# Key splits of an attention and MoE kernel: from a planner's choice of three engines to ScalarE and VectorE

## The chip, the cores and the metric

The kernel runs on one core of a Trainium2 chip. The metric is device time in microseconds (us) from one launch; the profile adds one execution with a record of every instruction. A core has TensorE (PE, matrix products; PEld is its loading of weights), VectorE (DVE), ScalarE (ACT), GpSimd (POOL) and SyncE (SP), each with its own queue of instructions, which it works off in order. SP here does nothing but issue DMAs.

## What is computed

An attention with a learned bias, followed by two feed-forward layers. The part that the change touches, cut down:

```python
scores = q @ k.T / 8                                   # 2 batches x 8 heads, 576 x 576, head size 64
x = log1p(abs(i - j)) / log1p(max(i, 1))               # for each query i and key j
bias = relu(x * w1 + b1) @ w2                          # 32 hidden units, one bias for each head
attn = softmax(scores + bias)
out = attn @ v
# then: two layers g(x @ w_in) @ w_out on 1152 tokens, model size 512, inner size 2048
```

All is float32. Where the kernel multiplies in the fp32r format of TensorE, it splits a number into a first part (rounded to fp32r) and a remainder, and adds up the products of the parts.

## The kernel before

**Stages.** One loop over steps from -16 to 83 issues the attention. In each step, functions that were put on a list for that step (`at` for a fixed engine, `flex` for a choice of engines) are issued by priority; the matrix products and the DMAs of a step come last. Then a second loop issues the two feed-forward layers. The order on every engine is thus written out ahead; the engines wait for one another by semaphores alone.

**The planner.** `flex` gives a cost for each engine that may do a piece of work (V is VectorE, A ScalarE, G GpSimd). `pick` (line 99) takes the engine whose load plus that cost is lowest, and adds the cost to the load. At the head of each step `run_step` (line 107) lowers each load by a pace (0.846 before step 0, 1.791 from it on), not below zero. A load that is carried along therefore shifts later choices too.

**Bias rows.** `bias_rows` (line 184) makes the bias for groups of 16 query rows. `relu` computes four hidden tiles of 128 x 576 (VectorE line 208, or ScalarE line 206), `mm` multiplies them by w2 on TensorE (line 219, eight products), `evac` brings the result from PSUM to a buffer (`copy`, ScalarE line 134 or VectorE line 142), and `store` sends it off by DMA. The first twelve groups ("near", the ones with start steps up to 2) fill two SBUF tiles `bias0`; the other 24 go through DRAM (`bd`) and have shorter tiles. There are nine buffers for hidden tiles, and two PSUM buffers for the first eight groups, which the score tiles share.

**Key splits.** `split_k` (line 275) does this for each of 8 heads and 2 batches: `hi` copies 64 partitions x 576 of the raw keys to fp32r (GpSimd line 144, ScalarE line 134 or VectorE line 138), and in the next step `lo` subtracts that copy from the raw keys (GpSimd or VectorE, line 149) and writes the remainder to the other 64 partitions. The raw keys come in four DMAs (`kraw`). `split_q` does the like for the queries, by the planner's choice on GpSimd.

**Scores.** From step 0 on, one tile of 128 queries and one head per step: TensorE makes the scores (line 364), VectorE adds the bias and takes the minimum of the negated scores (line 373), ScalarE takes exp (line 378), VectorE the reciprocal of the sum, GpSimd multiplies by it (`norm`, line 146), TensorE transposes (line 404), ScalarE copies that out of PSUM, and TensorE multiplies by v (lines 417 and 420). In the late steps weights of the feed-forward layers are split as well (`conv`, stages s0 to s4, lines 492 to 520).

Of the kernel before, what the change touches and what calls it, by code (L numbers as in the profile page):

```python
# [27 lines left out]
def f(ap):  # L28
    return ap.bitcast(F32)
# [5 lines left out]
def near_row(pr, m):  # L35

    return 64 * (pr // 4) + pr % 4 + 4 * m


class Kernel:  # L40
# [50 lines left out]
    def at(self, step, eng, fn, pri=0, cost=0.3):  # L91

        self.todo.setdefault(step, []).append((pri, eng, fn, cost))
# [90 lines left out]
    def bias_rows(self, pr, s0, p, ps, pss, cfg):  # L184


        nc = self.nc
        V, A, G, at = nc.vector, nc.scalar, nc.gpsimd, self.at
        i0 = 16 * pr
        near = pr < 12  # L190
        d = S if near else max(S - i0, i0 + 16)
        nh = 1 if d <= 512 else 2
        w = d // nh
        one = near and PAR["order"].index(pr) < PAR["ns"]
        st = {}
        hid = []
        c0 = i0 + 15

        def relu(e, j):
            t = p.tile([128, S], F32, tag="hid", name="hid", bufs=cfg["hid"])  # L200
            hid.append(t)
            thr = self.thr[:, 4 * pr + j:4 * pr + j + 1]
            o = 188 - near_row(pr, 4 * j)
            u = self.us[:, o:o + S] if near else self.u
            if e == "A":
                A.activation(t[:, :d], u[:, :d], AF.Relu, bias=thr)
            else:
                V.tensor_scalar(t[:, :d], u[:, :d], thr, 0.0, ALU.add, ALU.max)  # L208

        def mm(x):  # L210
            if one:
                if x == 0:
                    st["s"] = pss.tile([128, 2, 512], F32, tag="s", name="bps2", bufs=2)
                st[x] = st["s"][:, x]
            else:
                st[x] = ps.tile([128, 512], F32, tag="T", name="bps", bufs=3)
            w2 = self.w2s.rearrange("p i h -> p (i h)")
            for j in range(4):
                nc.tensor.matmul(st[x][32 * j:32 * j + 32, :w], lhsT=w2, rhs=hid[j][:, x * w:x * w + w],  # L219
                                 start=True, stop=True, tile_position=(0, 32 * j))  # L220

        def evac(e, x):
            if x == 0:
                st["buf"] = p.tile([128, BW], F32, tag="bbuf", name="bbuf", bufs=PAR["bbuf"])
            buf = st["buf"]
            if one:
                self.copy(e, buf[:, 0:d].rearrange("p (x c) -> p x c", x=2), st["s"][:, :, :w], self.rpsi[:, pr:pr + 1])
                return
            dst = buf[:, 0:d] if near else buf[:, c0:c0 + d] if i0 < 288 else buf[:, 0:d][:, ::-1]
            self.copy(e, dst[:, x * w:x * w + w], st[x][:, :w], self.rpsi[:, pr:pr + 1])  # L230

        n = c0 if i0 < 288 else 575 - i0

        def mirror(e):
            buf = st["buf"]
            if i0 < 288:
                self.copy(e, buf[:, 0:n], buf[:, c0 + 1:c0 + 1 + n][:, ::-1])
            else:
                self.copy(e, buf[:, c0 + 1:c0 + 1 + n], buf[:, c0 - n:c0][:, ::-1])

        def store():
            if near:
                for b in (0, 64) if pr < 4 else (64 * (pr >= 8),):
                    nc.sync.dma_start(self.bias0[pr >= 4][b + pr % 4:b + 64:4], st["buf"][:, 0:S])
                return
            bk, r = divmod(pr - 4, 8)
            dst = self.bd[bk][16 * r:16 * r + 16].rearrange("i h c -> (i h) c")
            nc.sync.dma_start(dst[:, 0:591], st["buf"][:, 0:591])

        for j in range(4):  # L250
            self.flex(s0, dict(V=PAR['rV'] + 0.52e-3 * d, A=PAR['rA'] + 0.83e-3 * d), lambda e, j=j: relu(e, j), PAR['vp'][6])
        for x in range(nh):
            g = 0 if one else x
            at(s0 + 1 + g, "P", lambda x=x: mm(x), PAR["pp"][1])
            if not one or x:
                v = d if one else w
                self.flex(s0 + (PAR["evd"][pr] if near else 2) + g, dict(V=0.13 + 1.04e-3 * v, A=0.1 + 0.83e-3 * v),
                          lambda e, x=0 if one else x: evac(e, x), PAR['vp'][7])
        if near:
            at(s0 + PAR["evd"][pr] + g, "end", store)  # L260
            return
        self.flex(s0 + 3 + g, dict(G=PAR['mG'] + 1e-3 * n, V=PAR['mV'] + 0.52e-3 * n, A=PAR['mA'] + 0.83e-3 * n), mirror, PAR['vp'][8])
        at(s0 + 4 + g, "end", store)
# [11 lines left out]
    def split_k(self, h, sl, s0, p, K, tag, bufs):  # L275


        nc, at = self.nc, self.at
        mine = slice(64 * (h % 2), 64 * (h % 2) + 64)
        other = slice(64 - 64 * (h % 2), 128 - 64 * (h % 2))  # L280

        def load():
            self.kraw[h // 2] = p.tile([128, B, S], F32, tag=tag, name="kraw", bufs=bufs)
            nc.sync.dma_start(self.kraw[h // 2], self.a["kc"][h // 2])

        def hi(e, b):
            self.copy(e, K[h][mine, b], self.kraw[h // 2][mine, b])

        def lo(e, b):
            self.sub(e, K[h][other, b], self.kraw[h // 2][mine, b], f(K[h][mine, b]))  # L290

        if h % 2 == 0:
            at(sl, "end", load, -1)
        for b in range(B):
            self.flex(s0 + b, dict(G=PAR['kG'], A=PAR['kA'], V=PAR['kV']), lambda e, b=b: hi(e, b), PAR['pe_'][4])
            self.flex(s0 + b + 1, dict(G=PAR['k2G'], V=PAR['k2V']), lambda e, b=b: lo(e, b), PAR['pe_'][4])

    def ring(self, name):

# [575 lines left out]
```

## Time and profile before

| | |
|---|---|
| median of 3 runs | 626.24 us (625.48 to 626.54) |
| profiled execution, its own time | 623.83 us |
| span of its records | 621.8 us |
| busy in the span | PE 590.9, DVE 514.9, ACT 411.5, POOL 408.1 us |

The span runs from the first to the last record. The profiled execution is a run of its own, so its time differs from the median of the others.

### The profile page before, as it was taken

To read this page: it belongs to the slowest core of one execution; us is meant where nothing else is said; L and a number is where in the kernel's file an instruction comes from. 1 tells how busy PE (TensorE), PEld (TensorE's weight loads), DVE (VectorE), ACT (ScalarE), POOL (GpSimd) and SP (SyncE) were. 2 spreads that over 40 slices of the span, in tenths; PEclk is the share of its full clock that TensorE was granted. 3 is DMA by queue.
4 is the path that set the end of the run, shared out by engine and by line. 5 is a ranking of instruction groups with operands and counts; after the bars stand their busy time and mean duration, and the time that the engine had idled before them with its cause. 6 is when DMAs were issued, how large, how long until landed. Compare 5 with 4: busy or idle time off the path is not lost.

```text
span 621.8 us, 11331 instructions
## 1 busy us (share of the span) xinstructions
PE 590.9 (95%) x4084; PEld 538.0 (87%) x4084; DVE 514.9 (83%) x963; ACT 411.5 (66%) x888; POOL 408.1 (66%) x427
## 2 busy tenths in 40 slices
PE   4679999999989879999999999999999999999997
PEld 1247777677878779999999999999999999999997
DVE  7998898989769779799999987999997699594432
ACT  4478787888778689888887877744754454543330
POOL 5867666686769468688999877665665476295220
PEclk9899999999999889999999999999999999999999
DMA  6876336665454302132212111232232122010012
GB/s 209 218 196 203 113 116 189 229 213 162 163 193 154 137 4 69 34 103 71 100 69 102 69 67 35 72 113 87 78 126 74 64 101 102 2 69 1 14 52 89
DMA packets 26888, 66.25 MB, mean 107 GB/s; under 512 B 4689, under 2 KB 6609, under 8 KB 26833
## 3 DMA queue, kind: packets, MB, share of 16 engines
q1 hardware_dynamic: 26688, 65.44, 32.1%
q8 instruction: 32, 0.52, 0.3%
q14 instruction: 24, 0.19, 0.1%
q10 hardware_dynamic: 144, 0.10, 0.1%
HBM read 51.19 MB, written 9.62 MB: 98 GB/s over the span
## 4 chain that ended last, share of the span: by engine, by line
PE 71%; DVE 16%; DMA 6%; issue 2%; ACT 2%; POOL 0%; SPq 0%; DVEq 0%; ACTq 0%; POOLq 0%
PE outps L733 30%; PE inps L690 29%; DVE hid L208 5%; PE tps L404 3%; PE vps L420 3%; PE sps L364 3%; PE bps L219 3%; DMA bias<-bd 3%; DVE P L373 2%; DVE wc L498 2%; DMA raw<-w 1%; DVE wc L502 1%; DVE K L149 1%; DMA qraw<-qt 1%; PE vps L417 1%
## 5 line engine op out<-in xcount | busy, mean ns | idle before, releaser
L733 PE MATMUL outps<-gh,wo 128*128 128x384 f32 x768 | 209.5, 335 | 0.0
L596 POOL TENSOR_TENSOR gl<-v,gh 128x384 fp32r<-128x384 f32 x96 | 110.0, 1147 | 79.0 <-ACT gh L592 74.5
L733 PEld LDWEIGHTS outps<-gh,wo 128*128 128x128 f32 x768 | 139.8, 188 | 0.0
L733 PE MATMUL outps<-gl,wo 128*128 128x384 f32 x384 | 128.3, 334 | 0.0
L690 PE MATMUL inps<-x,wh 128*128 128x384 f32 x384 | 100.4, 343 | 3.3 <-DVE x L439 2.0
L146 POOL TENSOR_SCALAR P<-P,m 128x576 f32<-128x576 f32 x72 | 59.6, 831 | 34.9 <-DVE m L383 25.2
L690 PEld LDWEIGHTS inps<-x,wh 128*128 128x128 f32 x384 | 70.7, 192 | 4.3 <-DVE x L439 2.3
L733 PEld LDWEIGHTS outps<-gl,wo 128*128 128x128 f32 x384 | 72.1, 188 | 0.0
L559 ACT ACTIVATE v<-inps,cst 128x384 f32<-128x384 f32 x48 | 27.8, 579 | 66.4 <-PE inps L690 63.5
L378 ACT ACTIVATE P<-P,m 128x576 f32<-128x576 f32 x72 | 56.1, 779 | 21.6 <-DVE m L373 21.2
L583 DVE SCALAR_TENSOR_TENSOR v<-v 128x384 f32<-128x384 f32 x48 | 39.8, 829 | 33.9 <-ACT v L559 33.6
L690 PE MATMUL inps<-x2l,wh 128*128 128x384 f32 x192 | 64.6, 337 | 1.6 <-DVE x2l L666 1.6
L563 POOL TENSOR_TENSOR q<-h,q 128x384 f32<-128x384 f32 x48 | 48.8, 1016 | 26.1 <-ACT q L556 25.7
L364 PE MATMUL sps<-K,Q 128*128 128x288 f32 x320 | 60.2, 314 | 5.6 <-DVE m L373 5.6
L690 PE MATMUL inps<-x,wl 128*128 128x384 f32 x192 | 65.3, 340 | 0.0
L690 PE MATMUL inps<-x2h,wh 128*128 128x384 f32 x192 | 64.7, 337 | 0.0
L690 PE MATMUL inps<-x2h,wl 128*128 128x384 f32 x192 | 64.5, 336 | 0.0
L592 ACT ACTIVATE gh<-v 128x384 fp32r<-128x384 f32 x96 | 50.7, 528 | 20.4 <-DVE v L584 19.2
L219 PE MATMUL bps<-hid,w2s 128*32 128x288 f32 (+17 forms) x416 | 48.8, 478 | 14.2 <-DVE hid L208 12.5
L502 DVE SCALAR_TENSOR_TENSOR wc<-raw,wc 128x512 int32<-128x512 int32 x64 | 61.3, 968 | 0.0
L373 DVE CUSTOM_DVE_ANT_0 P<-sps,bias 128x576 f32<-128x576 f32 x72 | 53.3, 747 | 9.1 <-DMA bias<-bd 6.6
L364 PEld LDWEIGHTS sps<-K,Q 128*128 128x128 f32 x320 | 45.0, 189 | 9.6 <-DVE m L373 5.7
(87 smaller groups left out, 1305.3 us busy)
## 6 DMA issues: line engine op xcount, KB each, us to landing
raw<-w SPq DMA_DIRECT2D x64, 512.0 KB
bd<-bbuf SPq DMA_DIRECT2D x24, 295.5 KB
bias<-bd SPq DMA_DIRECT2D x24, 288.0 KB
bias<-bbuf SPq DMA_DIRECT2D x16, 288.0 KB
qraw<-qm SPq DMA_DIRECT2D x16, 256.0 KB
V<-v SPq DMA_DIRECT2D x8, 320.0 KB
kraw<-kc SPq DMA_DIRECT2D x4, 576.0 KB
out<-acc SPq DMA_DIRECT2D x12, 192.0 KB
```

The costliest lines, as they stand in the source:

```text
L146: nc.gpsimd.tensor_scalar(out, x, scale, 1.0, ALU.mult, ALU.mult)
L219: nc.tensor.matmul(st[x][32 * j:32 * j + 32, :w], lhsT=w2, rhs=hid[j][:, x * w:x * w + w], start=True, stop=True, tile_position=(0, 32 * j))
L364: PE.matmul(x_[:, x, :288], lhsT=lhs, rhs=K[h][:, bb, 288 * x:288 * x + 288], start=(j == 0), stop=(j == len(seq) - 1))
L373: V.tensor_tensor_reduce(halves(o), S_.pop(t)[:, :, :288], halves(bt), -0.125, 3e38, ALU.add, ALU.min, sums[i][:, 0, e:e + 1])
L378: A.activation(s, s, AF.Exp, bias=m[:, 0, e:e + 1], scale=-1.0, accum_out=m[:, 1, e:e + 1])
L502: return [(dict(V=0.7), lambda e: V.scalar_tensor_tensor(tc, words[:, :, 0], 29, tc, ALU.logical_shift_right, ALU.bitwise_or))]
L563: return [lambda: G.tensor_tensor(o["q"], o["h2"], o["q"], ALU.add)] if m == 0 else []
L583: return [lambda: V.scalar_tensor_tensor(v, v, 1.0, v, ALU.min, ALU.mult), lambda: V.tensor_tensor(v, v, h2, ALU.add)]
L592: return [lambda: A.activation(gh, o["v"], AF.Copy)]
L596: return [lambda: G.tensor_tensor(gl, o["v"], f(o["gh"]), ALU.subtract)]
L690: nc.tensor.matmul(ps[:, :U], lhsT=w[:, c], rhs=y[:, c], start=(t == 0), stop=(t == 11))
L733: nc.tensor.matmul(ps[:, :U], lhsT=w[:, c], rhs=y, start=(t == 0), stop=(t == 11))
```

## The change

The key splits lose their choice of engine: all sixteen `hi` go to ScalarE and all sixteen `lo` to VectorE, each entered in the planner with 0.68. For the relus of groups with a start step of at most 2, which are the twelve near groups, the planner's costs become 0.51 on VectorE and 0.77 on ScalarE, in place of 0.43 and 0.91 (0.13 + 0.00052 x 576 and 0.427 + 0.00083 x 576).

```diff
         for j in range(4):
-            self.flex(s0, dict(V=PAR['rV'] + 0.52e-3 * d, A=PAR['rA'] + 0.83e-3 * d), lambda e, j=j: relu(e, j), PAR['vp'][6])
+            c = dict(V=PAR['rV'] + 0.52e-3 * d, A=PAR['rA'] + 0.83e-3 * d) if s0 > 2 else dict(V=0.51, A=0.77)
+            self.flex(s0, c, lambda e, j=j: relu(e, j), PAR['vp'][6])
...
         for b in range(B):
-            self.flex(s0 + b, dict(G=PAR['kG'], A=PAR['kA'], V=PAR['kV']), lambda e, b=b: hi(e, b), PAR['pe_'][4])
-            self.flex(s0 + b + 1, dict(G=PAR['k2G'], V=PAR['k2V']), lambda e, b=b: lo(e, b), PAR['pe_'][4])
+            self.flex(s0 + b, dict(A=0.68), lambda e, b=b: hi(e, b), PAR['pe_'][4])
+            self.flex(s0 + b + 1, dict(V=0.68), lambda e, b=b: lo(e, b), PAR['pe_'][4])
```

Before, the planner's costs for the splits were G 0.377, A 0.407, V 0.204 for `hi`, and G 1.36, V 0.456 for `lo`.

## Rows read from the trace of the kernel before

**Rows 1.** Windows: start:end and length, busy time (count) by engine, PE clock, DMA share, GB/s.

```profile
4.00:28.00 24.00, 15.05 (x106) 5.36 (x110) 23.53 (x29) 10.14 (x15) 19.76 (x20) 0.93 0.78 216
28.00:49.00 21.00, 17.61 (x158) 9.71 (x155) 20.62 (x40) 16.70 (x37) 13.71 (x20) 1.00 0.79 215
...
53.00:100.00 47.00, 46.65 (x508) 36.17 (x508) 40.62 (x109) 37.41 (x92) 29.68 (x42) 1.00 0.45 153
100.00:162.00 62.00, 60.56 (x576) 44.02 (x575) 54.61 (x144) 49.33 (x120) 42.81 (x57) 1.00 0.55 178
162.00:186.00 24.00, 22.00 (x217) 19.61 (x216) 17.21 (x47) 19.75 (x53) 16.74 (x20) 1.00 0.58 203
186.00:212.00 26.00, 23.74 (x222) 20.76 (x222) 22.66 (x49) 19.34 (x48) 18.07 (x18) 0.98 0.47 159
...
234.00:392.00 158.00, 158.00 (x909) 158.00 (x907) 141.05 (x265) 130.11 (x270) 129.04 (x127) 1.00 0.22 74
```

**Rows 2.** Chain that ended last, 0 to 125 us: start, length, what.

```profile
20.00 3.23 DVE hid L208 x2
...
50.61 2.47 DVE hid L208 x3
...
53.90 0.48 PE tps L404 x3
```

**Rows 3.** Groups by line and shape, 0 to 125 us: count, busy us, mean ns.

```profile
L208 DVE TENSOR_SCALAR hid<-us,thr 128x576 f32<-128x576 f32 x36 | 27.5, 829 | 0.2
L373 DVE CUSTOM_DVE_ANT_0 P<-sps,bias 128x576 f32<-128x576 f32 x37 | 27.4, 746 | 2.6 <-PE sps L364 1.7 <-DMA bias<-bd 0.8
...
L149 POOL TENSOR_TENSOR K<-kraw,K 64x576 fp32r<-64x576 f32 x9 | 13.3, 1475 | 3.0 <-ACT K L134 2.3
...
L144 POOL TENSOR_SCALAR K<-kraw 64x576 fp32r<-64x576 f32 x12 | 10.5, 877 | 6.8 <-DMA kraw<-kc 6.1
L206 ACT ACTIVATE hid<-us,thr 128x576 f32<-128x576 f32 x12 | 9.1, 766 | 4.1 <-DVE thr L176 3.1 <-PE bps L219 1.0
L149 DVE TENSOR_TENSOR K<-kraw,K 64x576 fp32r<-64x576 f32 x7 | 8.5, 1209 | 0.2
...
L134 ACT ACTIVATE bbuf<-bps,small 128x576 f32<-128x576 f32 x8 | 5.9, 740 | 13.5 <-PE bps L219 13.4
...
L149 POOL TENSOR_TENSOR Q<-qraw,Q 128x128 fp32r<-128x128 f32 x8 | 5.1, 657 | 0.0
...
L144 POOL TENSOR_SCALAR Q<-qraw 128x128 fp32r<-128x128 f32 x8 | 3.4, 438 | 1.9 <-DMA qraw<-qt 1.7
...
L134 ACT ACTIVATE K<-kraw 64x576 fp32r<-64x576 f32 x3 | 2.0, 675 | 0.0
...
L142 DVE TENSOR_SCALAR bbuf<-bps,small 128x304 f32<-128x304 f32 x2 | 1.1, 530 | 0.1
```

**Rows 4.** Instructions on the hidden tiles, 0 to 125 us: ns minimum, median, maximum.

```profile
L208 DVE TENSOR_SCALAR hid<-us,thr x36: 500/704/1660, 5.5 to 37.5; 128x576 f32<-128x576 f32 x36
```

**Rows 5.** The same columns for the instructions on the key tiles, 0 to 60 us.

```profile
L149 DVE TENSOR_TENSOR K<-kraw,K x7: 753/1103/1849, 13.0 to 48.4; 64x576 fp32r<-64x576 f32 x7
```

**Rows 6.** VectorE in order of time: start, length, what, count.

```profile
19.26 8.57 DVE L208 TENSOR_SCALAR hid<-us,thr 128x576 f32<-128x576 f32 x9
...
28.59 6.30 DVE L208 TENSOR_SCALAR hid<-us,thr 128x576 f32<-128x576 f32 x12
...
48.36 0.75 DVE L149 TENSOR_TENSOR K<-kraw,K 64x576 fp32r<-64x576 f32 x1
49.14 0.61 DVE L382 TENSOR_SCALAR m<-m 128x2 f32<-128x2 f32 x1
...
180.19 1.65 DVE L149 TENSOR_TENSOR wo<-wc,wo 128x512 fp32r<-128x512 f32 x1
```

**Rows 7.** GpSimd in order of time; in brackets the idle time before it.

```profile
178.69 0.62 POOL L144 TENSOR_SCALAR wo<-wc 128x512 fp32r<-128x512 f32 x1 [3.43 <-DVE m L382]
...
189.93 1.28 POOL L149 TENSOR_TENSOR wo<-wc,wo 128x512 fp32r<-128x512 f32 x1
```

## The prediction

> **What bounds the kernel now.** I first cut the span into stretches by what the engines do [rows 1]. From 53 to 162 us TensorE is busy 46.65 of 47 and 60.56 of 62 us, and again without a gap from 234 to 392. Those stretches start when TensorE gets its first work and then take the time that they take; nothing in the change makes them shorter. Before them it is otherwise: from 4 to 49 us TensorE has gaps, and VectorE is busy 23.53 of 24 and 20.62 of 21 us, 44.15 of 45 in all. ScalarE has 26.84 us of work there and GpSimd 33.47. The chain that ended last says the same: it runs through VectorE's relus up to 53.08 us and passes to TensorE at 53.90 [rows 2]. So the head of the kernel costs what VectorE has queued there, and a microsecond taken off that queue lets all the rest start a microsecond sooner.
>
> Then I asked why VectorE is so full. The 36 near relus occupy it for 27.5 us, 764 ns apiece [rows 3], though the shortest takes 500 ns and the longest 1660 [rows 4]. The length follows GpSimd: nine of them took 8.57 us from 19.26, and twelve took 6.30 us from 28.59 [rows 6], and GpSimd is busy 82% of the time from 4 to 28 us and 65% from 28 to 49 [rows 1]. The remainders on VectorE show it too, from 753 to 1849 ns for one shape [rows 5]. Of GpSimd's work in that head 23.8 us (13.3 + 10.5) are key splits [rows 3].
>
> **Who does what after the change.** I followed the planner's sums from step -16 on with both sets of costs. For the kernel before they give 36 near relus on VectorE and 12 on ScalarE, `hi` 12 on GpSimd, 3 on ScalarE, 1 on VectorE, `lo` 9 on GpSimd and 7 on VectorE, as the trace has them [rows 3]. With the new costs they give 32 and 16 near relus, sixteen `hi` on ScalarE, sixteen `lo` on VectorE, and, since the loads are now higher, four `evac` that move to VectorE (two of 128x576, two of 128x288). Query splits, `norm` and mirrors stay on GpSimd. Later the hidden tiles of the far groups change hands about evenly (two fewer on VectorE), two transposes are copied out by VectorE, and in steps 58 to 74 five stages of the weight splits move from VectorE to GpSimd. From step 75 on the three loads are the same number in both, so the two feed-forward layers are issued alike.
>
> **VectorE's queue in the head, step by step.** It runs from the first relu at 5.5 us [rows 4] to the last key remainder, which ends at 48.36 + 0.75 = 49.11 [rows 6].
> - Near relus: 27.5 us before. After, 32 of them. With GpSimd still they take 0.50 less the overlap of one with the next (829 - 764 = 65 ns), 0.435; the twelve from 28.59 show 0.525 with GpSimd working most of that time. I take 0.50, as only query splits are left: 16.0, saved 11.5. Bounds: 13.9 to 16.8, saved 13.6 to 10.7.
> - Remainders: 7 for 8.5 us before. After, 16. The one at 48.36 frees the engine at 49.14, so 0.78 each; bounds 0.753 and the median of before, 1.103 [rows 5, 6]. I take 0.80, nearest to the undisturbed one, 12.8: cost 4.3, bounds 3.5 to 9.1.
> - The four `evac`: no 576-wide one on VectorE is shown; the bias add (line 373) reads as many elements from PSUM in 0.746, and a 304-wide `evac` takes 0.530 [rows 3]. 2 x 0.75 + 2 x 0.50 = 2.5; bounds 2.1 (by 0.530 each) and 3.0 (by 0.746 each).
> - One `hi` fewer on VectorE: between nothing and the shortest relu, 0.5. I take 0.5.
>
> Sum: 11.5 - 4.3 - 2.5 + 0.5 = 5.2 us saved; by the good ends 13.6 - 3.5 - 2.1 + 0.5 = 8.5, by the bad ends 10.7 - 9.1 - 3.0 + 0 = -1.4.
>
> **What the shift puts on ScalarE, and new waits.** Thirteen `hi` more at 0.675, four relus at 0.766, four `evac` fewer (two at 0.740, two at some 0.48): 8.8 + 3.1 - 2.4 = 9.5 us [rows 3]. 26.8 + 9.5 = 36.3 us of work must fit into some 40. It does, as 13.4 us of ScalarE's idle time were `evac` waiting for bias products that waited for VectorE's relus [rows 3], and these come sooner. Behind a `hi` that waits for its raw keys, relus and `evac` now queue, and a `lo` on VectorE waits for a `hi` one step earlier. Adding up both queues in issue order with the times above, I find ScalarE within a microsecond of VectorE throughout, so I charge 0.5 us for such waits; bounds 0 and what the second rival says. The first `hi` waited on GpSimd for its raw keys [rows 3]; on ScalarE three relus come before it, 2.3 us at 0.766, which cover what is left of that wait. DMAs: 0.78 x 24 + 0.79 x 21 = 35.3 us of busy share in the head [rows 1]; squeezed into 40 us that is 88%, which leaves room, and the stores are issued earlier with their `evac`. I count nothing for it; full DMA queues would end the head at 4 + 35.3 us at the earliest, sooner than VectorE does.
>
> **The late stages.** Five stages leave VectorE, among them one that took 1.65 us beside GpSimd [rows 6], and add 4 x 1.28 + 0.62 = 5.7 us to GpSimd, whose work from 162 to 212 us is 34.8 of 50 [rows 1, 7]. One falls where GpSimd sat idle for 3.43 us [rows 7]. `norm` is issued before them in each step, but the next step's `norm` queues behind them, and TensorE's transposes wait for that. VectorE, 22.66 of 26 us busy from 186 on, gains what GpSimd loses. I count 0, within 1.5 either way.
>
> **Total.** 5.2 - 0.5 = 4.7 us sooner into the full stretch of TensorE, and carried to the end. The durations are from the profiled execution, 623.83 us by its own time (span 621.8 and 2.0 around it), so that one would become 619.1; the median of the runs is 2.4 above it, so 626.24 - 4.7 = 621.5.
>
> **A rule of the skill beside the rows.** The rows say that a near relu took 0.500 at best and 0.525 as a mean over a stretch in which GpSimd worked 65% of the time, so a GpSimd instruction stretches only some of VectorE's [rows 1, 4, 6]. The Trainium skill, SBUF — State Buffer, section "Who interferes with whom", says that the two engines share a port pair as an exclusive lock, held for a whole instruction, and that a VectorE operation with two inputs in SBUF contends too. It fits the maximum of 1660 ns, and by it the query splits that stay on GpSimd can still hold VectorE up; that is the third rival.
>
> **Rivals.**
> 1. *Both engines full, no waits, remainders and relus at their undisturbed lengths.* 8.5 us saved, 617.7. For it: GpSimd's work in the head falls from 33.5 to under 10 us. Against it: two queues that cross at every bias group seldom run without waits. Chance 0.17.
> 2. *ScalarE becomes the bound (the other side).* If its 13.4 us of waits for bias products stay, since each group still goes relu, product, `evac` over three engines, its head takes 36.3 + 13.4 = 49.7 us in place of 45: 4.7 us later, 630.9. It decides against the change where more than 8.7 of the 13.4 us stay. Against it: those waits had VectorE's relus as their cause. Chance 0.07.
> 3. *The remaining query splits hold VectorE up for all their time.* Four units cost 5.1 + 3.4 = 8.5 us of GpSimd [rows 3]. Undisturbed, the saving is 8.5; less 8.5 it is nothing, 626.2. Against it: the stretch from 28.59 held query splits and still gave 0.525 per relu. Chance 0.10.
> 4. *The gain is partly given back*, by remainders at 0.95 (2.4 us more) or by late `norm`s in steps 58 to 74 (1.5): 4.7 - 2.4 = 2.3, 623.9. Chance 0.14.
>
> **Chances and range.** My forecast, 3.2 to 6.7 us saved, has 0.52. Under 0.2% (1.25 us) a measurement of this kernel can't tell a change from none. Faster by more: 0.52 + 0.17 + 0.14 = 0.83; within: 0.10; slower: 0.07. The range takes in the first, and the fourth rival with the bad end of its price: 617.5 to 625.0.
>
> **What would show it.** In the profile after: near relus 32 on VectorE with a mean near 0.55 (right) or still above 0.7 (rival 3); `lo` 16 times near 0.8; `hi` 16 times at 0.675; the last key remainder ends at about 44.4 us, not 49.1; the first transposes (line 404) at about 44 and TensorE without gaps from about 49; ScalarE's waits for bias products well under 8.7 us. From about 157 us on the same DMA waits for the bias as before at 162, and the feed-forward layers with their lengths unchanged, 4.7 us earlier. Wrong would be: ScalarE without idle time while VectorE waits for `hi`; transposes that wait for `norm` behind weight splits on GpSimd; or an earlier start that is lost again at the bias loads between 162 and 186 us.

## The result, and the profile after

The changed kernel took 619.48 us (median of 4 runs, 618.80 to 620.36), the kernel before on the same chip 625.86 (4 runs, 623.61 to 626.54): ratio 0.9908, 95% interval 0.9887 to 0.9929. So it is 0.7 to 1.1% faster. The forecast was 621.5. The profiled execution went from 623.83 to 618.80 us by its own time, its span from 621.8 to 617.0, so 4.8 us came off the span where 4.7 were forecast. That is one execution of each kernel. The medians lie 6.4 us apart (4.4 to 7.1 by the interval), and 5.7 in a repetition (e12), so the gain is nearer 6 us than the 4.7 of the forecast.

The windows of the kernel after, with the columns of [rows 1]:

```profile
4.00:28.00 24.00, 17.07 (x144) 7.89 (x144) 21.52 (x43) 20.71 (x32) 2.70 (x4) 1.00 0.90 242
28.00:49.00 21.00, 18.63 (x149) 11.44 (x148) 19.41 (x41) 19.35 (x43) 13.30 (x20) 0.92 0.83 230
...
53.00:100.00 47.00, 46.77 (x499) 36.13 (x499) 41.32 (x109) 37.14 (x92) 29.30 (x41) 1.00 0.43 142
100.00:162.00 62.00, 60.53 (x574) 44.43 (x573) 54.27 (x142) 49.88 (x124) 42.91 (x56) 1.00 0.56 177
162.00:186.00 24.00, 22.60 (x230) 20.10 (x230) 17.24 (x50) 19.63 (x51) 19.36 (x23) 1.00 0.62 211
186.00:212.00 26.00, 23.08 (x191) 20.97 (x189) 21.13 (x42) 18.97 (x44) 19.32 (x19) 0.93 0.43 136
...
234.00:392.00 158.00, 158.00 (x909) 158.00 (x908) 140.59 (x266) 129.96 (x269) 128.88 (x126) 1.00 0.22 71
```

Against [rows 1], GpSimd has almost left the first 24 us (19.76 to 2.70 us), ScalarE has filled up (10.14 to 20.71), and VectorE, the engine that bounded the head, now has gaps (busy 21.52 us for 23.53, and 19.41 for 20.62). From 53 us on little differs.

The groups from 0 to 125 us, which answer to [rows 3]:

```profile
L208 DVE TENSOR_SCALAR hid<-us,thr 128x576 f32<-128x576 f32 x32 | 14.7, 520 | 1.1 <-PE bps L219 1.0
...
L149 DVE TENSOR_TENSOR K<-kraw,K 64x576 fp32r<-64x576 f32 x16 | 12.9, 805 | 0.5
...
L206 ACT ACTIVATE hid<-us,thr 128x576 f32<-128x576 f32 x16 | 11.8, 768 | 4.6 <-DVE thr L176 3.1 <-PE bps L219 1.5
...
L134 ACT ACTIVATE K<-kraw 64x576 fp32r<-64x576 f32 x16 | 10.8, 678 | 0.3
...
L134 ACT ACTIVATE bbuf<-bps,small 128x576 f32<-128x576 f32 x6 | 4.4, 739 | 1.2 <-PE bps L219 1.1
```

The counts are those that the planner's sums had given: 32 and 16 near relus, sixteen `hi`, sixteen `lo`, six of eight wide `evac` left on ScalarE. A near relu on VectorE fell from 829 to 520 ns as a mean, and all of them together from 27.5 us to 14.7.

How VectorE's queue came out is read from its order of time after the change:

```profile
9.09 0.82 DVE L142 TENSOR_SCALAR bbuf<-bps,small 128x576 f32<-128x576 f32 x1 [1.36 <-PE bps L219]
...
17.97 0.82 DVE L142 TENSOR_SCALAR bbuf<-bps,small 128x576 f32<-128x576 f32 x1 [0.39 <-PE bps L219]
...
29.00 0.99 DVE L208 TENSOR_SCALAR hid<-us,thr 128x576 f32<-128x576 f32 x2 [0.98 <-PE bps L219]
...
44.22 0.83 DVE L149 TENSOR_TENSOR K<-kraw,K 64x576 fp32r<-64x576 f32 x1
```

The last remainder ends at 44.22 + 0.83 = 45.05 us, 4.06 before the 49.11 of [rows 6]. Ahead of it stand waits that were not there: two `evac`, moved to VectorE, wait for bias products, and a relu waits for one of the nine hidden buffers. How much that is shows in two windows, each from the first relu to the end of the last remainder. The kernel before:

```profile
5.40:49.11 43.71, 32.77 (x260) 15.18 (x261) 43.21 (x64) 26.66 (x52) 33.58 (x39) 0.96 0.77 210
```

and after:

```profile
5.40:45.05 39.65, 31.74 (x262) 16.53 (x263) 36.17 (x71) 36.26 (x67) 12.04 (x19) 0.96 0.86 230
```

VectorE's work fell by 43.21 - 36.17 = 7.04 us, and its idle time grew from 0.50 to 39.65 - 36.17 = 3.48 us: 2.98 of the 7.04 us went into new idle time, 2.73 of them into the three waits shown (1.36 + 0.39 + 0.98), the rest into short gaps between instructions. ScalarE, at 36.26 of 39.65 us, is now as full as VectorE.

TensorE in order of time, where the scores begin:

```profile
36.06 0.69 PE L219 MATMUL bps<-hid,w2s 128*32 128x288 f32 x8 [1.86 <-ACT bbuf L134]
36.94 1.65 PE L365 MATMUL sps<-K,Q 128*128 128x288 f32 x8 [0.19 <-DVE m L374]
...
39.64 2.00 PE L365 MATMUL sps<-K,Q 128*128 128x288 f32 x8
...
44.37 0.55 PE L405 MATMUL tps<-late,P 128*128 128x128 f32 x3
```

The first transposes start at 44.37 us, 48.70 before, and the first products with v at 49.84, 54.76 before. From there the lead of 4.9 us stays: the first score tiles of the next stretches start 4.85 us (71.88 for 76.73) and 4.8 us (106.14 for 110.95) earlier, the first product of the second feed-forward matrix 4.8 (230.7 for 235.5), the end 4.8. This is read from one execution of each; in e12, the changed kernel once more, that product starts at 232.2 us.

The chain that ended last leaves VectorE sooner than the prediction had it. In the kernel before it runs through VectorE up to 53.08 us [rows 2]. After the change it passes to TensorE here:

```profile
36.80 0.10 DVE m L374
...
36.94 1.65 PE sps L365 x8
...
44.44 0.48 PE tps L405 x3
```

From there TensorE has no gap up to 60 us (in e4 and e12 one of 0.2 us near 47), where before the last one ended at 53.12:

```profile
36.94:60.00 23.06, 23.06 (x212) 16.17 (x212) 21.41 (x51) 19.49 (x47) 14.28 (x20) 0.93 0.74 226
```

So the transposes, which start before the last remainder has ended, follow TensorE's own work there, and the end of VectorE's remainders is no longer what sets their start.

### The profile page after: what moved, and what is told of

It reads as the page before. It is cut to its first block, busy times and chain, and to the rows that moved or that the text cites. A ratio compares the mean times of both kernels' runs of the same rounds, so it can differ in the third digit from the quotient of the medians.

```text
span 617.0 us, 11315 instructions
## 1 busy us (share of the span) xinstructions
PE 589.2 (95%) x4084; PEld 539.0 (87%) x4084; DVE 505.4 (82%) x967; ACT 420.6 (68%) x900; POOL 391.1 (63%) x411
## 4 chain that ended last, share of the span: by engine, by line
PE 74%; DVE 13%; DMA 6%; ACT 2%; issue 2%; POOL 1%; SPq 0%; DVEq 0%; POOLq 0%; ACTq 0%
PE outps L734 30%; PE inps L691 29%; PE bps L219 4%; PE sps L365 4%; PE tps L405 4%; PE vps L421 3%; DMA bias<-bd 3%; DVE hid L208 2%; DVE wc L503 2%; DVE wc L499 1%; DMA bias<-bbuf 1%; DVE P L374 1%; PE vps L418 1%; DVE K L149 1%; DMA raw<-w 1%
## 5 line engine op out<-in xcount | busy, mean ns | idle before, releaser
L146 POOL TENSOR_SCALAR P<-P,m 128x576 f32<-128x576 f32 x72 | 58.1, 810 | 36.3 <-DVE m L384 27.5
L374 DVE CUSTOM_DVE_ANT_0 P<-sps,bias 128x576 f32<-128x576 f32 x72 | 53.4, 747 | 10.8 <-DMA bias<-bd 4.8
L219 PE MATMUL bps<-hid,w2s 128*32 128x288 f32 (+17 forms) x416 | 46.5, 472 | 13.4 <-DVE hid L208 10.9
L405 PE MATMUL tps<-late,P 128*128 128x128 f32 x324 | 50.9, 284 | 3.5 <-POOL P L146 2.9
```

The source lines that it names most:

```text
L146: nc.gpsimd.tensor_scalar(out, x, scale, 1.0, ALU.mult, ALU.mult)
L374: V.tensor_tensor_reduce(halves(o), S_.pop(t)[:, :, :288], halves(bt), -0.125, 3e38, ALU.add, ALU.min, sums[i][:, 0, e:e + 1])
L405: PE.transpose(t[:, 128 * j:128 * j + 128], Pf()[:, 384 * c + 128 * j:384 * c + 128 * j + 128], self.ident)
```

## The experiments

The theory: GpSimd's key splits stretch VectorE's relus and remainders, VectorE's queue sets the start of TensorE's full stretch, and that lead lasts to the end. Its rivals: the relus' new shares do it; ScalarE had become the bound or was about to; the late stages, which the planner's loads shift, make or take some of it. Each edit stands against the changed kernel.

**The two halves of the change (e1, e2).** e1 keeps the splits and takes the old relu costs:

```diff
-c = dict(V=PAR['rV'] + 0.52e-3 * d, A=PAR['rA'] + 0.83e-3 * d) if s0 > 2 else dict(V=0.51, A=0.77)
+c = dict(V=PAR['rV'] + 0.52e-3 * d, A=PAR['rA'] + 0.83e-3 * d)
```

> Only the key splits move (hi to ScalarE, lo to VectorE); the relu costs are those of before. Theory (VectorE's queue is shorter because GpSimd no longer stretches its instructions): the planner now puts 34 near relus on VectorE and 5 evac, two relus and one evac more than in the changed kernel, 2 x 0.46 + 0.5 = 1.4 us, so about 1.4 us less gained: ratio to before near 0.993, near relus near 0.52 us each. Rival (the relu costs bring the gain): ratio near 1.000.

Measured: 621.09 us, ratio 0.9942 (0.9929 to 0.9955). The last remainder ends at 45.20 us, relus took 522 ns (34 of them). So the head is as short as with the whole change. I had charged 1.4 us for two relus and an `evac` more on VectorE; from 5.40 to 45.20 us it did have 37.98 us of work for 36.17, but its idle time fell to 1.82 us from 3.48, so the ratio came near the forecast for another reason. The interval touches that of the changed kernel. If the 0.3% between them is real, it is lost behind the head: the first products with v start at 49.81 us (49.84 in the changed kernel), that of the second feed-forward matrix at 232.9 (230.7, and 232.2 in e12).

e2 keeps the relu costs and gives the splits back their choice:

```diff
-self.flex(s0 + b, dict(A=0.68), lambda e, b=b: hi(e, b), PAR['pe_'][4])
-self.flex(s0 + b + 1, dict(V=0.68), lambda e, b=b: lo(e, b), PAR['pe_'][4])
+self.flex(s0 + b, dict(G=PAR['kG'], A=PAR['kA'], V=PAR['kV']), lambda e, b=b: hi(e, b), PAR['pe_'][4])
+self.flex(s0 + b + 1, dict(G=PAR['k2G'], V=PAR['k2V']), lambda e, b=b: lo(e, b), PAR['pe_'][4])
```

> Only the relu costs change; the planner then puts 31 near relus on VectorE, 13 hi and 10 lo on GpSimd. Theory: GpSimd's share stays, so a near relu stays near 0.77 us; 5 relus fewer on VectorE save 3.8 us and one lo fewer 1.2, two evac more cost 1.2, and GpSimd's extra split stretches what is left: 1 to 3 us gained, ratio 0.995 to 0.998. Rival (the relu costs bring the gain): ratio near 0.991.

Measured: 623.99 us, ratio 0.9983 (0.9963 to 1.0002). The groups of e2, 0 to 125 us:

```profile
L208 DVE TENSOR_SCALAR hid<-us,thr 128x576 f32<-128x576 f32 x31 | 26.5, 918 | 0.6 <-PE bps L219 0.5
L149 POOL TENSOR_TENSOR K<-kraw,K 64x576 fp32r<-64x576 f32 x10 | 14.8, 1481 | 4.7 <-ACT K L134 4.0
```

Five relus fewer than before on VectorE, and yet 26.5 us against 27.5: each of those that stayed grew from 829 to 918 ns. What was saved in number was paid back in length, since GpSimd had as much to do as ever. I had expected relus near 0.77 us and 1 to 3 us saved; by the interval it is from nothing to 2.3 us.

**GpSimd's work put back, with nobody waiting for it (e3).** The changed kernel with 12 copies and 9 subtractions of the splits' size on GpSimd, from the raw keys into tiles that are never read:

```diff
+self.scr = [near.tile([128, S], F32R, name=f"scr{i}") for i in range(2)]
...
+raw = self.kraw[h // 2][mine, b]
+if h < 6:
+    self.copy("G", self.scr[0][mine], raw)
+if b == 0 or h == 0:
+    self.sub("G", self.scr[1][mine], raw, raw)
```

> The changed kernel, and beside it GpSimd does 12 copies and 9 subtractions of 64x576 on raw keys into scratch that nobody reads, as many as its key splits were before. Theory (shared access stretches VectorE's instructions): near relus back to a mean of 0.75 us or more, remainders to 1.1, so 32 x 0.25 + 16 x 0.3 = 13 us more on VectorE: slower than before, ratio near 1.01. Rival (the gain is only that work moved from late GpSimd and VectorE queues to an idle ScalarE): relus stay at 0.52, ratio stays near 0.991.

Measured: 631.14 us (2 runs), ratio 1.0104 (1.0083 to 1.0126), slower than the kernel before; the last remainder ends at 56.36 us, 11.3 later than in the changed kernel, and the first product of the second feed-forward matrix starts 11.3 us later too (242.05 for 230.72). The groups of e3:

```profile
L209 DVE TENSOR_SCALAR hid<-us,thr 128x576 f32<-128x576 f32 x32 | 22.3, 756 | 1.1 <-PE bps L220 1.0
L149 DVE TENSOR_TENSOR K<-kraw,K 64x576 fp32r<-64x576 f32 x16 | 15.7, 980 | 0.5
L149 POOL TENSOR_TENSOR scr<-kraw 64x576 fp32r<-64x576 f32 x9 | 12.0, 1331 | 0.4
...
L144 POOL TENSOR_SCALAR scr<-kraw 64x576 fp32r<-64x576 f32 x12 | 11.1, 926 | 6.4 <-DMA kraw<-kc 5.7
```

Shape and number on VectorE are those of the changed kernel; only the lengths differ: relus 22.3 us for 14.7, remainders 15.7 for 12.9. So 12.0 + 11.1 = 23.1 us of GpSimd cost VectorE 7.6 + 2.8 = 10.4 us, 0.45 for each. This shows the cause that the theory names, apart from everything else in the change.

The traces say the same relu by relu. In the kernel before, e2, e3, e5 and e6 the near relus during which GpSimd worked on nothing (9, 7, 12, 13 and 18 of them) took 500 to 521 ns; the longest of each kernel took 1660, 1666, 1407, 928 and 1677.

**Which half of a split must leave GpSimd (e6, e5).** e6 puts the remainders back on GpSimd, e5 the first parts:

```diff
-self.flex(s0 + b + 1, dict(V=0.68), lambda e, b=b: lo(e, b), PAR['pe_'][4])     # e6
+self.flex(s0 + b + 1, dict(G=1.36), lambda e, b=b: lo(e, b), PAR['pe_'][4])
...
-self.flex(s0 + b, dict(A=0.68), lambda e, b=b: hi(e, b), PAR['pe_'][4])         # e5
+self.flex(s0 + b, dict(G=0.68), lambda e, b=b: hi(e, b), PAR['pe_'][4])
```

> The changed kernel with all sixteen remainders on GpSimd (16 x 1.4 = 22 us there) and the first parts on ScalarE; the planner then puts 33 near relus and 11 evac on VectorE. Theory (0.45 us for each us of GpSimd): 12.9 us of remainders leave VectorE, 10 us of stretching and 4.5 us of evac and relu come, so VectorE's head ends about 1.6 us later than in the changed kernel: ratio to before near 0.993, near relus near 0.75. Rival (a GpSimd instruction holds VectorE up for its full length): 22 + 4.5 - 12.9 = 14 us later, ratio near 1.013.

> The changed kernel with all sixteen first parts on GpSimd (16 x 0.88 = 14 us there) and the remainders on VectorE; the planner then puts 25 near relus on VectorE. Theory (each microsecond of GpSimd costs VectorE about 0.45 us: 10.4 us more for 23.1 us of scratch work in the run with scratch work): 14 x 0.45 = 6.3 us more, seven relus and one evac fewer 4.1 us less, so the last key remainder ends near 47.3 us, ratio to before near 0.994. Rival (only GpSimd instructions with two inputs get in VectorE's way): near relus stay at 0.52, ratio 0.986 or lower.

e6 took 624.01 us, ratio 0.9999 (0.9982 to 1.0017); the last remainder, on GpSimd, ends at 50.10 us. Its groups:

```profile
L208 DVE TENSOR_SCALAR hid<-us,thr 128x576 f32<-128x576 f32 x33 | 25.5, 833 | 0.6 <-PE bps L219 0.6
L149 POOL TENSOR_TENSOR K<-kraw,K 64x576 fp32r<-64x576 f32 x16 | 23.4, 1465 | 17.0 <-ACT K L134 13.3 <-issue 2.7
```

Here 23.4 us of subtractions stretched 33 relus by (833 - 520) x 33 = 10.3 us, 0.44 for each. With the remainders on GpSimd nothing is gained. I had expected 0.993, with VectorE 1.6 us behind the changed kernel, so this forecast missed; by the same short row (line 383) it was 4.4 us behind, 49.49 for 45.08. The stretching came as expected (10 us), but VectorE also took two first parts of the queries (1.53 us, line 138), and a row of `u` (line 182) took 1.67 us there for 0.52; neither was in the sum. Nor is VectorE alone in the way here: a `norm` queues behind the last remainder on GpSimd (50.20 us), and the transposes wait 0.39 us for it.

e5 took 618.70 us, ratio 0.9906 (0.9884 to 0.9928), the same as the changed kernel. I had expected it slower, so that forecast failed. Its groups:

```profile
L149 DVE TENSOR_TENSOR K<-kraw,K 64x576 fp32r<-64x576 f32 x16 | 14.5, 907 | 0.5
L208 DVE TENSOR_SCALAR hid<-us,thr 128x576 f32<-128x576 f32 x25 | 14.5, 629 | 0.2
L144 POOL TENSOR_SCALAR K<-kraw 64x576 fp32r<-64x576 f32 x16 | 13.8, 861 | 7.8 <-DMA kraw<-kc 6.7
```

13.8 us of copies stretched VectorE by (629 - 520) x 25 + (907 - 805) x 16 = 4.4 us, 0.32 for each. Against that ScalarE, freed of 10.8 us, took 23 near relus in place of 16, and VectorE 25 in place of 32. The last remainder ended at 42.65 us, 2.4 sooner than in the changed kernel, though VectorE had no less to do:

```profile
5.40:42.65 37.25, 31.13 (x263) 15.56 (x264) 36.44 (x62) 30.80 (x60) 24.99 (x35) 1.00 0.89 238
...
L142 DVE TENSOR_SCALAR bbuf<-bps,small 128x576 f32<-128x576 f32 x2 | 1.6, 808 | 0.0
```

Its work is 36.44 us for 36.17, its idle time 0.81 for 3.48: the 2.4 us are the new waits, gone, and VectorE has two wide `evac` here too. My sum for e5 had not counted on that. So the gain of the change sits in the remainders that left GpSimd; the first parts need not have left.

**Waits for hidden buffers, and what the loads carry (e4, e8, e9).** e4 sets the planner's loads at step 13 to what they are there in the kernel before, so that the later steps choose as that one does; e9 is e1 with the same line; e8 is e4 with four more hidden buffers in a pool of their own:

```diff
+if s == 13:                                        # e4, e8, e9
+    self.load = dict(V=3.739, A=3.489, G=0.0)
...
-t = p.tile([128, S], F32, tag="hid", name="hid", bufs=cfg["hid"])
+t = (self.nearp.tile([128, S], F32, tag="hidn", name="hidn", bufs=4) if near and j == 0 else   # e8
+     p.tile([128, S], F32, tag="hid", name="hid", bufs=cfg["hid"]))
```

> The changed kernel, with the planner's three loads set at step 13 to what they are there in the kernel before, so that from then on every choice is that of before (the five weight stages stay on VectorE, two transposes stay with ScalarE). Theory (late stages are worth about nothing): ratio to before 0.989 to 0.993, the same as the changed kernel's within 1.5 us. Rival (the five stages on GpSimd give part of the gain back, as TensorE now waits for norm for 2.2 us near 200 us): 1 to 2 us faster than the changed kernel, ratio near 0.988. Rival (VectorE's relief in the late steps is part of the gain): 1 to 2 us slower than it, ratio near 0.993.

> The changed kernel with the loads set as before at step 13, and four more buffers for the first hidden tile of each near group, so that a group's relus wait for the product three groups back instead of two. Theory (of the 2.5 us that VectorE now waits in the head, 1.0 us are waits of relus for a free hidden buffer, and 1.5 us on ScalarE): up to 1 us faster than the kernel with the loads set alone, ratio to before 0.989 to 0.991. Rival (TensorE's order of score and bias products sets the pace there, not the buffers): waits for bias products turn up at the evac instead, ratio 0.991.

> Only the key splits move, the relu costs are those of before, and the loads are set at step 13 to those of the kernel before, so that later choices are its own. In the run with the splits alone the head ended as early as in the changed kernel (45.2 against 45.05 us), yet the end came 2.2 us later. Theory (those 2.2 us come from later choices that the carried loads change, by chance): ratio to before 0.990 to 0.992, as the changed kernel. Rival (the near relus' sharing itself is worth 2 us, felt after 50 us): ratio near 0.994 again.

e4: 618.99 us, ratio 0.9907 (0.9892 to 0.9922), as the changed kernel: the other choices of the late stages are worth nothing that stands out of an interval of 1 us either way, as forecast. e9: 619.82 us, 0.9929 (0.9912 to 0.9946), between e1 and e4, and its interval touches both, so what e1 lost behind the head is not settled.

e8: 617.54 us, 0.9889 (0.9872 to 0.9907), span 614.7 against 617.2 of e4; I had allowed it 1 us. Its window up to the end of its last remainder:

```profile
5.40:43.71 38.31, 30.82 (x264) 16.30 (x265) 35.84 (x71) 35.96 (x67) 10.41 (x19) 1.00 0.90 238
```

VectorE is idle for 38.31 - 35.84 = 2.47 us there, 1.0 less than in the changed kernel, and the last remainder ends 1.3 us sooner. The wait for hidden buffers is gone, and it was about a third of the new idle time. But e8 and e4 differ in more than that: the granted TensorE clock from 28 to 49 us was 1.00 in e8 and 0.92 in e4, and the interval overlaps that of e4. So the 2.5 us are not shown to be the buffers' (see e13).

**The better split, and whether the differences are larger than one execution (e10 to e13).** e10 is e5 with the line of e4, e11 is that with the buffers of e8:

```diff
-self.flex(s0 + b, dict(A=0.68), lambda e, b=b: hi(e, b), PAR['pe_'][4])          # e10, e11, e13
+self.flex(s0 + b, dict(G=0.68), lambda e, b=b: hi(e, b), PAR['pe_'][4])
```

> The changed kernel with the first parts of the key tiles on GpSimd instead of ScalarE (remainders stay on VectorE), and the loads of the choice set back at step 13 to what they are there in the kernel before, so that the later stages choose as that one does. Run e5 had the head end 2.4 us earlier than the changed kernel and lost it again between 156 and 195 us. Theory A, the choices carried over by the loads lose it: last remainder ends near 42.7 us, first output matmuls near 228.5 us, ratio near 0.987. Theory B, the bias loads and the norms between 156 and 195 us end that stretch whenever it begins: first output matmuls again near 230.5 us, ratio near 0.9905.

> As e10, and four further hidden buffers for the near tiles of the first slot, as in run e8 (which was 2.5 us of span faster than the same kernel without them). If what e5 gained in the head and what e8 gained there are separate and both last: last remainder ends near 41.5 us, first output matmuls near 227 us, ratio 0.984 to 0.986. If they are the same waits, removed twice, or the stretch between 156 and 195 us takes back what comes early: head as in e8 (43 us) or earlier, first output matmuls 228 to 230 us, ratio 0.988 to 0.990.

e10: 617.13 us, 0.9879 (0.9860 to 0.9899), first product of the second feed-forward matrix at 228.2 us, as theory A had it. e11: 617.19 us, 0.9881 (0.9861 to 0.9900): the two gains do not add. Its last remainder ends at 43.35 us, no sooner than in e10, and VectorE now waits 2.0 us for first parts on GpSimd. The interval of e10 overlaps that of the changed kernel, so both were run again side by side, unchanged:

> The changed kernel itself, beside run e13 on one chip, since the intervals of the changed kernel and of e10 overlap. Both theories: ratio 0.990 to 0.992, last remainder near 45 us, first output matmuls near 231 us.

> The kernel of e10 itself (first parts on GpSimd, remainders on VectorE, loads set back at step 13), beside e12 on one chip. If moving the remainders alone is the better half of the change: ratio 0.987 to 0.989, 0.3% under e12, with non-overlapping intervals, last remainder near 43 us, first output matmuls near 228 us. If the 2.7 us of e10 from the bias waits between 156 and 195 us were chance of one chip or one execution: ratio within 0.15% of e12 and first output matmuls near 230.5 us although the head ends at 43 us.

e12 (the changed kernel): 619.33 us, 0.9905 (0.9881 to 0.9930). e13 (the kernel of e10): 618.48 us, 0.9888 (0.9867 to 0.9909). It was ahead again, but by 0.17% and with intervals that overlap: neither forecast came out cleanly, and that e10 beats the changed kernel is likely, not shown. The traces of e10 and e13, one kernel twice, say why. TensorE in e10:

```profile
35.50 1.32 PE L367 MATMUL sps<-K,Q 128*128 128x288 f32 x8 [2.16 <-DVE m L376]
...
38.36 1.29 PE L367 MATMUL sps<-K,Q 128*128 128x288 f32 x8 [0.92 <-DVE m L376]
...
42.38 0.55 PE L407 MATMUL tps<-late,P 128*128 128x128 f32 x3
```

and in e13:

```profile
35.19 1.32 PE L367 MATMUL sps<-K,Q 128*128 128x288 f32 x8 [1.72 <-DVE m L376]
...
38.05 2.26 PE L367 MATMUL sps<-K,Q 128*128 128x288 f32 x8 [0.64 <-DVE m L376]
...
41.68 2.16 PE L367 MATMUL sps<-K,Q 128*128 128x288 f32 x8
...
44.52 0.55 PE L407 MATMUL tps<-late,P 128*128 128x128 f32 x3
```

The last remainder ends at 43.26 us in the one and 42.94 in the other, yet the transposes start 2.1 us apart. In e13 the score products of 1.3 us took 2.2 us from 38 to 44 us, after gaps of the same kind in both. The granted clock from 37 to 44 us was 0.53 in e13, so nearly all of it at 1.2 GHz, and 1.00 in e10, at 2.4 GHz. Later the bias loads differ too. Waits of e10 from 156 to 195 us (total, count, longest):

```profile
DVE P L376 <- DMA bias<-bd: 1.9, 2, 1.6
```

and of e13:

```profile
DVE P L376 <- DMA bias<-bd: 7.2, 4, 3.4
```

So a single execution moves by 2 us between the head and 195 us with nothing changed. What I read as "lost again between 156 and 195 us" in e5, and as the loads' doing in e10, is within that; theory A of e10 is not borne out by e13. What stays is the end of the last remainder, some 2 us sooner in e5, e10 and e13 than in the changed kernel (45.05, and 45.56 in e12). That these 2 us are carried on is not shown: the first products with v start at 47.42, 48.05 and 49.43 us there, at 49.84 and 50.34 in the changed kernel, and the time of none of these runs is clear of the changed kernel's.

## Why the prediction was right

**VectorE's queue in the head was the bound, and GpSimd stretched it.** Shown, by e3: GpSimd's work alone, with no one waiting for it, lengthens the head by 11.3 us, and the stretch of TensorE behind it starts as much later. e2 and e6 agree. It holds for the kernel before. After the change VectorE shares the bound: TensorE runs without gaps not from about 49 us, as the prediction had it, but from 36.94, and e5's head, 2.4 us shorter still, brought no time that can be told from the changed kernel's.

**The relus.** Forecast 0.50 each and 11.5 us saved; measured 14.7 us for 32, so 0.46 each, and 27.5 - 14.7 = 12.8 saved, between my value and the good end (13.6). The query splits, for whose sake I took 0.50, hardly touched them: their raw queries landed only at 22.85 and 28.80 us, and from 4 to 28 us GpSimd worked 2.70 us in all. That also ends the third rival; its sign, relus still above 0.7 us, did not come (0.52).

One reading behind the 0.50 was wrong. The prediction took 0.525 from twelve relus "with GpSimd working most of that time", and by 65%, which is the share from 28 to 49 us. In their own stretch GpSimd worked 2.96 of 6.30 us, 47%:

```profile
28.59:34.89 6.30, 6.10 (x54) 3.15 (x53) 6.20 (x13) 4.72 (x9) 2.96 (x5) 1.00 0.99 247
```

So 0.525 was no bad end for relus beside a busy GpSimd; e2's 26.5 us for 31, 0.85 each, is nearer to one. It did no harm here because GpSimd was idle while 25 of the 32 near relus ran.

**The remainders.** 0.80 and a cost of 4.3 us forecast, 0.805 and 12.9 - 8.5 = 4.4 measured. The four `evac` cost 2 x 0.82 + 2 x 0.51 = 2.66 where 2.5 was put: the wide one is slower than the bias add (0.746) by which I sized it. With half a microsecond for the `hi`, the work saved by these rows is 6.2 us, and 7.04 by the busy time of the whole queue, against 5.2 in the sum. What the sum left out is a row of `u` that fell from 0.92 to 0.52 us, and one relu of a far group fewer.

**The new waits are the term that was mis-sized.** I charged 0.5 us because adding up both queues put ScalarE within a microsecond of VectorE; VectorE's idle time grew by 2.98. Waits on VectorE in the kernel after, 4 to 45 us:

```profile
DVE bbuf L142 <- PE bps L219: 1.8, 2, 1.4
DVE hid L208 <- PE bps L219: 1.0, 1, 1.0
```

That sum priced the four moved `evac` as work alone. But an `evac` waits for products that wait for relus of both engines, and on VectorE such a wait stands in the queue that sets the end. Whether it waits depends on the rest: in e5, with the first parts off ScalarE (30.80 us of work in 37.25, for 36.26 in 39.65), VectorE has two wide `evac` as well and waits for none. So the likely cause is ScalarE, filled with first parts; but the planner gave VectorE the `evac` of other groups there (the first at 16.39 us, not 9.09), and the two are not separated. The other wait is that for the ring of nine hidden buffers, of which the sum knew nothing; in e8, with thirteen, that wait is gone and the one for the products stands (1.7 us). Work better than forecast by 1.8 us and waits worse by 2.5 nearly cancel, which is why 4.06 us at the last remainder lies 0.6 under the 4.7 of the sum (45.05 against the 44.4 us named). So the 4.7 was right for a reason that is partly luck. So is the match of 4.8 with 4.7 at the end of the profiled executions: the medians fell by 6.4 us, 1.7 more than the sum, with 4.7 inside the interval, and which term would hold the difference is open.

**ScalarE (second rival).** Work of 36.3 us was forecast, 36.26 measured. It fits, because its waits for bias products fell from 13.4 to

```profile
ACT bbuf L134 <- PE bps L219: 1.4, 3, 0.9
```

as the prediction had it. But it fits with nothing to spare, and TensorE feels it. Its gap of 1.86 us before 36.06 was for an `evac` that stood on ScalarE behind two first parts and an exp:

```profile
33.47 1.39 ACT L134 ACTIVATE K<-kraw 64x576 fp32r<-64x576 f32 x2
34.77 0.76 ACT L379 ACTIVATE P<-P,m 128x576 f32<-128x576 f32 x1
...
35.53 0.87 ACT L134 ACTIVATE bbuf<-bps,small 128x288 f32<-128x288 f32 x2
```

After it the score products took 1.65 and 2.00 us in place of 1.3, at a granted clock of 0.69 from 36.9 to 42.4 us. e1 had this gap at 1.17 us and a clock of 1.00 there: its transposes start at 43.42 us, 0.95 sooner, but its first products with v at the same time (49.81), so up to there it cost nothing. e5, as fast with the first parts on GpSimd, shows that those on ScalarE cost about as much as they bring.

**No waits, 8.5 us (first rival).** Excluded: the work came within 1.5 us of it, the waits took 3.

**Partly given back (fourth rival).** Not seen. Remainders of 0.805 exclude its first cause. Its second can be seen in VectorE's order of time after,

```profile
163.04 0.76 DVE L374 CUSTOM_DVE_ANT_0 P<-sps,bias 128x576 f32<-128x576 f32 x1 [0.69 <-DMA bias<-bd]
...
179.45 0.76 DVE L374 CUSTOM_DVE_ANT_0 P<-sps,bias 128x576 f32<-128x576 f32 x1 [2.59 <-POOL P L146]
...
188.62 0.76 DVE L374 CUSTOM_DVE_ANT_0 P<-sps,bias 128x576 f32<-128x576 f32 x1 [1.22 <-DMA bias<-bd]
```

where a score tile at 179 us waits behind a `norm`; but VectorE's waits for the bias loads were no longer than before (4.8 us for 6.6 over the whole execution, a figure that e10 and e13 show to move by more than that), and the lead is 4.9 us at the first products with v and 4.8 us from 230 us on. The forecast of 0 within 1.5 holds, and e4 agrees.

**The rule of the skill.** The Trainium skill, SBUF — State Buffer, section "Who interferes with whom", has one engine blocked while the other holds the shared ports. e3, e5 and e6 put a size to it for these shapes: 0.32 us of VectorE for a microsecond of copies on GpSimd, 0.44 to 0.45 where subtractions are among them. On average that is a part of GpSimd's time, as the prediction took from the relus of [rows 6]. One relu by itself can wait for most of a subtraction: the longest of e6 took 1677 ns, 1.2 us above the shortest, beside subtractions of 1465.

## What to carry to other kernels

When two engines slow each other, price a move by what it does to the lengths of the other engine's instructions: here moving relus away from VectorE brought 0.2%, not clear of noise (those left grew from 829 to 918 ns), and moving GpSimd's subtractions to VectorE as well, where they are more work for the bounding engine, another 0.8% (e5 against e2). When a planner's costs change, look at what else moves to the bounding engine, and ask of each such piece whether it waits for other engines; a piece that costs 0.8 us can hold the queue for another 1.4. When one engine's queue gets shorter, look for the engine that bounds next; here the chain that ended last left VectorE 16 us sooner. And before a difference of 2 us between two profiles is given a cause, profile one kernel twice.

## What the runs showed of the hardware that was not expected

- TensorE's clock in the head is not the kernel's alone. After a gap of 1.7 to 2.2 us near 34 us, score products of 1.3 us went on at 1.3 in e10 (granted clock 1.00 from 37 to 44 us) and took 2.2 in e13 (0.53), the same kernel; the changed kernel had 1.65 and 2.00 after a gap of 1.86, with 0.92 from 28 to 49 us in all three profiles of this order (itself, e4, e12). The first transposes of e10 and e13 lie 2.1 us apart.
- A copy on GpSimd stretches VectorE by less than a subtraction does: 0.32 us for each microsecond (e5; 0.36 and 0.34 in e10 and e13) against 0.44 (e6). Counting only the time in which the two ran at once, the near relus of e5 grew by 3.2 us over 500 ns each in 7.2 us of copies (and 0.9 of subtractions), those of e6 by 11.0 us in 15.5 us of subtractions (and 1.3 of copies).
- The waits for the same bias loads between 156 and 195 us came to 1.9 us in one execution of a kernel and 7.2 in another. What sets them was not found.
